# Mish between an attention's exponentials: fp16 products in place of 32-bit fused steps, with new thresholds for the order

## The chip, the cores and the metric

The kernel runs on one core of a Trainium2 chip. The metric is the device time of one execution in microseconds (us), as a median over runs. Shorter is better.

## The reference, cut to what matters

```python
x = A_x                                             # (1, 2048, 640), bf16
g = sigmoid((x * gate_w).sum(-1, keepdims=True))
# A: full attention, 32 heads of 20
q, k, v = heads(x @ wqkv)
a = softmax(q @ k.T * 20 ** -0.5) @ v @ wo
# B: dense layer with Mish
h = x @ w1 + b1                                     # 640 -> 1536
sp = log1p(exp(-abs(h))) + where(h > 0, h, 0)
b = (h * tanh(sp)) @ w2                             # 1536 -> 640
out = g * a + (1 - g) * b
```

Mish is `h * tanh(softplus(h))`. All of it is over 2048 tokens.

## The kernel before

**The bulk of the work** is attention: 2048 tiles of 128 keys by 512 queries (4 chunks of queries, 32 heads, 16 blocks of keys). TensorE forms the scores of three tiles at a time in one half of PSUM (a slot; two halves take turns, L1163), ScalarE turns them into exponentials in SBUF (`emit_e`, L1185), and TensorE multiplies these with V (`pv`, L1422). There are 683 such slots.

**The third tile of a slot can go to VectorE instead** ("off-loaded", `choose`, `emit_x`). ScalarE then takes 1024 elements per partition in place of 1536. VectorE evicts the third tile from PSUM as a scaled integer (L1230), and when four such tiles of a group have come together, `close` lines up three steps for the batch: an AND/OR for the fraction (L1294), a product in fp16 (L1298, often as two halves) and an AND/OR for the power (L1302). TensorE multiplies both parts of such a batch with V.

**Dense layer B.** Its first product is cut into 48 tasks (`h_task`), one for 256 tokens and 256 of the 1536 features. VectorE adds the bias as it evicts (L936). Two tasks make one call of `mish` on 128 x 1024 elements, 24 calls in all. ScalarE forms a tanh into a 32-bit buffer U (L959). Then VectorE forms a polynomial in U, times h, by four fused 32-bit steps of the form (in0 + constant) * in1 (SCALAR_TENSOR_TENSOR, L977), with the buffer U2 between them; the result replaces h. U has one copy (it moves from the tile W2R to the tile REG once). It is marked "busy" from the tanh to the last of the four steps, and the next call's tanh is only issued after that. A factor MISH_BY that the polynomial leaves out is in OMG, the factor (1 - g) by which the second product is scaled (L992).

**The order of all instructions is worked out in Python** when the kernel is built, by the class `Plan` and the loop over slots at the end of `attention`. It keeps an estimated time for each engine, adds estimated costs (EXP, WIDE and so on), and decides greedily what comes next. Attention's slots have the lead. Tasks of the projections, of B and of the output are put between them on TensorE (`pick`, `put`); VectorE's work that isn't urgent stands in four kinds of queues (`norm`, two lanes of `soon` for the batches, `blend` for Mish, `bg`), and `work` takes what can begin first. `choose` off-loads a tile unless one of these stops it: VectorE's queue is over a bound (BEHIND, 8 us; after off-loaded slots in a row 5 and 4 us, and never four in a row), no buffer is free, or a batch could not be ready in time. The end of a batch is judged with the queue's length times CROWD. Tasks of B that lag behind their due slot by LAG or more bring the bound on the queue to SPARE (7 us).

The thresholds that the change touches: OWE (how much background work of TensorE may be owed before more is put between), STREAM (below which share of work TensorE repeats scores to stay busy), SPREAD (over how many slots a task with a deadline is spread), GAP (the wait before scores from which a task is put there), CROWD, EAGER (how far ahead of its due slot a task is taken when others can't run), MISH (VectorE's cost of a Mish per task, for the check of what must end in time), LAG and REFILL (how long before ScalarE needs them the next scores must be due).

Of the kernel before, what the change touches and what calls it, by code (L numbers as in the profile page):

```python
# [12 lines left out]
FP16 = mybir.dt.float16  # L13
AF = mybir.ActivationFunctionType
ALU = mybir.AluOpType
# [14 lines left out]
CW = 512  # L30
# [6 lines left out]
NETS = 6  # L37
OLD = 3
WAITED = 3
OWE = 0.6  # L40
SLOT = 3
PV_HOLD = 2
HALF = D // 2
# [9 lines left out]
COL = 1 / 2400.0  # L53
PASS = CW * COL
EXP = 1.335
STREAM = 0.48
SPUN = 0.65
EXP_PAIR = 0.908
WIDE = 0.60
FAST = 0.335  # L60
HALVED = 0.41
HALF_WORK = 0.6
# [14 lines left out]
QUAD = 0.60  # L77
DOUBLE = 1.134
AHEAD = 14
SPREAD = 2  # L80
GAP = 0.5
SLOW_LOAD = 5.0
EARLY = 4
BEHIND = 8
PATIENCE = 5
CATCH_UP = 5
BUSY = 0.6
CROWD = 1.6
MARGIN = 2.5
EAGER = 20  # L90
LOAD = 0.95
MISH = 2.25
GROUP = 2.2
LAST = 0
END = 45
SHIFT = 0.4
LAG = 25
SPARE = 7
WINDOW = 3.41
CALM = 3  # L100
# [6 lines left out]
H_AT = 150  # L107
H_STEP = 12.5
THIN = 0.09
REFILL = 0.66  # L110
OVER = 0.2
CUTS = ((0, 256), (256, 256))

# [5 lines left out]
ULPS = 1024 / math.log(2)  # L119
BIAS = 15 * 1024 + 436  # L120
LIFT = math.log(1.5069154) + 436 / ULPS
MISH_STEPS = (1.5274980615848066, -5.90257334954394, 18.967422148121276, -6.430071830749512)
MISH_BY = -0.006540836794009846
MISH_AT = 0.6830045149697055
MANTISSA = 0x3FF
EXPONENT = 0x7C00
HALVES = 0x3800
# [111 lines left out]
def bass_gated_mix__softmax_full_mha__dense_activation_mish__prompt_kernel(  # L239
# [19 lines left out]
    def sb(name, shape, dt):  # L259
        return st.enter_context(nc.sbuf_tensor(name, shape, dt))  # L260
# [20 lines left out]
    U2 = sb("U2", [P, 2 * CW], FP32)  # L281
# [8 lines left out]
    GATE = sb("GATE", [P, NTB], FP32)  # L290
    OMG = sb("OMG", [P, NTB], FP32)
# [90 lines left out]
    def attention(pl, fast):  # L382
# [56 lines left out]
        def dve(fn, deps=(), cost=0.1, kind="F"):  # L439

            ready = max([pl.now["dve"], *(d.t1 + HOP for d in deps if d is not None)])
            work(ready + (LATER if fast and now["rate"] < BUSY and now["bank"] else SLACK))
            return pl.add("dve", fn, deps, cost=cost, kind=kind)
# [72 lines left out]
        if fast:  # L516
# [73 lines left out]
            def kq_task(k, g, c, due, forced=True):  # L590
# [8 lines left out]
                def finish(bank, last):  # L599
# [4 lines left out]
                    to = dst[:, g, c * CW:(c + 1) * CW]  # L604
                    ev = dve(lambda e: e.tensor_copy(to, PS[:, bank, :]), [last], WIDE)
                    (q_done, k_done)[k][(g, c)] = ev
# [21 lines left out]
            def shelve(k, name, c, rows, src, ev, n, i=0):  # L628

                done = (q_done, k_done)[k]  # L630
                written[(k, name, c)] = moved = pl.add(
                    "sp", lambda e: e.dma_start((QS, KS)[k].ap()[c, rows, :], src), [ev], f"{'qk'[k]}w{n}{i}", cost=0.5)
                (wq_read, k_moved)[k].append(moved)
                stage_free.setdefault((k, n), []).append(moved)
                for g, names in needs_of.items():
                    if (g, c) not in done and name in names and all((k, m, c) in written for m in names):
                        done[(g, c)] = None
                        later(now["step"] + 3, lambda g=g, c=c, names=names: fetch(k, g, c, names))
# [20 lines left out]
            def pack_task(k, i, c, due):  # L659
# [8 lines left out]
                def finish(bank, last):  # L668
# [4 lines left out]
                    to = stages[k][n]  # L673
                    ev = dve(lambda e: e.tensor_copy(to, PS[:, bank, :]), [last, *stage_free.pop((k, n), ())], WIDE)
                    shelve(k, i, c, slice(base, base + P), to, ev, n)
# [9 lines left out]
            def pack_end_task(k, c, due):  # L685
# [9 lines left out]
                def finish(bank, last):  # L695
# [5 lines left out]
                    to = stages[k][n]  # L701
                    ev = dve(lambda e: e.tensor_copy(to, PS[:, bank, :]), [last, *stage_free.pop((k, n), ())], WIDE)
                    for i in range(2):
# [14 lines left out]
            def copy(eng, dst, src, dep, cost):  # L718
                if eng == "act":
                    return pl.add("act", lambda e: e.copy(dst, src), [dep], cost=cost + 0.04)  # L720
                return pl.add("dve", lambda e: e.tensor_copy(dst, src), [dep], cost=cost)
# [8 lines left out]
            def first_keys():  # L730
# [3 lines left out]
                def turn(f):  # L734
# [4 lines left out]
                    turned[:] = [last]  # L739
                    moved[f] = bank_free[f] = copy(("dve", "act")[f % 2], xt(0)[:, f, :], PS[:, f, :], last, WIDE)  # L740

# [10 lines left out]
                q, k = QT[:, 0, 0:CW], KT[:, 0, 0:CW]  # L752
                q_done[(0, 0)] = bank_free[5] = copy("dve", q, PS[:, 5, :], last, WIDE)
                k_done[(0, 0)] = bank_free[FB] = copy("act", k[:, lows], PS[:, FB, 0:HW], low, 0.36)
# [37 lines left out]
            def v_pair_task(g, tiles, due):  # L792
# [9 lines left out]
                def finish(bank, last):  # L802
                    for c in cs:
# [5 lines left out]
                        V_all[:, tiles[0]:tiles[0] + m, g * HG:(g + 2) * HG, 1:EW],  # L809
                        got[:, :, 0:2 * HD].rearrange("p t (h d) -> p t h d", d=DH)), [last, m_one], WIDE * m / 3)  # L810
                    v_done.update({(g + i, t): ev for t in tiles for i in range(2)})
# [9 lines left out]
            def sigmoid(got):  # L821
                ex = pl.add("act", lambda e: e.activation(GATE[:, :], GT1[:, :], AF.Exp, scale=-1.0), [got], cost=0.2)
                a = dve(lambda e: e.tensor_scalar_add(OMG[:, :], GATE[:, :], 1.0), [ex])
                r = dve(lambda e: e.reciprocal(GATE[:, :], OMG[:, :]), [a], 0.25)
                gate_done.append(dve(lambda e: e.tensor_scalar(
                    OMG[:, :], GATE[:, :], -MISH_BY, MISH_BY, ALU.mult, ALU.add), [r]))

            grams = {}
            guarded = []
# [85 lines left out]
            h_done, b_read = {}, {}  # L915
            u_free = [None]

            def h_task(hc, k, due):
# [25 lines left out]
                def ready():  # L944
                    if len(acts) > 1 or not guarded or n1 not in w1_load or (hc >= 2 and len(b_read.get(hc - 2, ())) < 4):
                        return None
                    if hc == 1 and not back(("h", 0)):
# [3 lines left out]
                return Task([mm(i, f) for i in range(2) for f in range(NFT)], HW * COL, finish, due, ready,  # L951
                            dve=WIDE + MISH)

            def mish(ev, hb, hc, k):


                h = hb.rearrange("p i t -> p (i t)")
                U = AREAS[6 * hc + k >= FIRST][2]
                ex = pl.add("act", lambda e: e.activation(U, h, AF.Tanh, scale=0.5, bias=-MISH_AT / 2), [ev, u_free[0]], cost=0.95)  # L959
                u_free[0] = "busy"  # L960
                last = [ex]
                due = ex.t1 + PATIENCE

                def piece(cost, fn, after=None):
                    def run():
                        last[0] = pl.add("dve", fn, [last[0]], cost=cost)
                        if after:
                            after(last[0])
                    blend.append((cost, run, lambda: last[0], due))

                def done(op):
                    u_free[0] = h_done[(hc, k - 1)] = h_done[(hc, k)] = op

                two = 2 * WIDE - 0.07
                steps = ((U2[:, :], U, U), (U2[:, :], U2[:, :], U), (U, U2[:, :], h), (h, U2[:, :], U))
                for n, (to, one, by) in enumerate(steps):
                    piece(two, lambda e, n=n, to=to, one=one, by=by: e.scalar_tensor_tensor(  # L977
                        to, one, MISH_STEPS[n], by, ALU.add, ALU.mult), done if n == 3 else None)

            def b_task(hc, t, half, due):  # L980
                c, part = divmod(hc, 2)
# [139 lines left out]
        def emit_s(s):  # L1121
# [7 lines left out]
            if fast and s >= EARLY:  # L1129
                ready = max(d.t1 + HOP for d in deps if d is not None)  # L1130
                while ready - pl.now["pe"] > GAP:
                    t = pick(ready)
# [191 lines left out]
        def choose(s):  # L1324
# [8 lines left out]
            def tight(group, need):  # L1333
                ends = max((i for i, v in enumerate(near) if v[:2] == group), default=0)
                left = ends / TAKEN * EXP
                before = sum(t[0] for t in blend if t[3] < pl.now["act"] + left)
                return (late + urgent + before) * CROWD + need + MARGIN >= left

# [187 lines left out]
        if fast:  # L1526
# [64 lines left out]
            done = 0.0  # L1591
# [39 lines left out]
        def pick(limit):  # L1631
# [7 lines left out]
            for t in tasks:  # L1639
                if begin + t.cost > limit or passed and t.due > now["step"] + EAGER:  # L1640
                    return None
# [30 lines left out]
        def room():  # L1672
# [4 lines left out]
            owing = sum(t.dve for t in tasks) + sum(t[0] for todo in (norm, *soon, blend, bg) for t in todo)  # L1677
            owing += 2 * MISH * len(acts) + GROUP * (len(order) // (NKT * HG) + 1) + CHAIN
            return owing + max(0.0, pl.now["dve"] - pl.now["act"]) < LOAD * (NSLOT - LAST - step) * EXP
# [25 lines left out]
        def fill_up(to_come, last):  # L1705
# [3 lines left out]
            while step < NSLOT and pl.streamed(upto - WINDOW) + to_come < SPUN * WINDOW:  # L1709
                short = pl.streamed(upto - WINDOW) + to_come < STREAM * WINDOW  # L1710
                free = bank_free.get(FB)
# [9 lines left out]
        for step in range(NSLOT + 40):  # L1721
# [3 lines left out]

            for t in [t for t in tasks if t.forced and t.due - SPREAD <= step]:
                share = t.left() / (max(0, t.due - step) + 1)
# [33 lines left out]
            if step + 2 < NSLOT:  # L1761
                compose(step + 2, choose(step + 2) if fast and step >= CALM and (step < slot_of(0, 1, 0) or behind < CATCH_UP and (lag < LAG or backlog() < SPARE) and room()) else None)
                emit_s(step + 2)
# [9 lines left out]
            if fast and step + 2 < NSLOT:  # L1773
                latest[0] = pl.now["act"] + sum(EXP_PAIR if s in off else EXP for s in (step + 1, step + 2)) - REFILL
                limit = min(limit, latest[0])
# [9 lines left out]

            while owed > (OWE if turn and fast and step < NSLOT else 0):
                t = pick(limit)
# [35 lines left out]
        for n, (bank, t, half) in enumerate(jobs):  # L1823
            tb = c * 4 + t
            dst = ended(t, half)
# [138 lines left out]
```

## Time and profile before

| | |
|---|---|
| median of 3 runs | 800.76 us (800.62 to 800.96) |
| the profiled execution | 800.83 us; its span in the trace 799.0 us |
| granted TensorE clock, mean | 0.997 |
| slots with three tiles on ScalarE / with two | 303 / 380 |
| Mish calls (tanh on ScalarE) | 24 |

How to read the lines that follow: a line names the kernel's line (L1185), the engine, the operation, the tile written and the tiles read, with partitions x elements and type, then a count, the time busy and the mean duration of one. PE is TensorE, PEld its weight loads, ACT ScalarE, DVE VectorE, SP the engine that issues most DMAs. A duration in the trace includes a start and an end that overlap with the neighbours on the same engine; the time that an instruction takes up is read from the distance of two starts.

### The profile page before, as it was taken

The numbers are of one execution on the slowest core, as the hardware profiler recorded it, in microseconds if no ns is written. First come the engines' busy times: TensorE is split into PE (matmuls) and PEld (weight loads), VectorE is DVE, ScalarE is ACT, GpSimd is POOL, SyncE is SP. The second block draws the span as 40 slices with busy tenths as digits, with TensorE's granted clock in tenths as the row PEclk, the third lists the DMA queues.
The fourth block names the chain that finished last, engine by engine and source line by source line (L and its number), as shares of the span: only waits on it lengthen the run. The fifth ranks groups of instructions, "written<-read, shape, count | busy, mean of one in ns | idle before, by whom it ended". The sixth has DMA issues, their size and how long they took to land.

```text
span 799.0 us, 16266 instructions
## 1 busy us (share of the span) xinstructions
PE 722.8 (90%) x6665; PEld 261.2 (33%) x6665; DVE 739.9 (93%) x1195; ACT 782.0 (98%) x714; POOL 7.3 (1%) x14
## 2 busy tenths in 40 slices
PE   8899999999988889999999989989889888989995
PEld 3333333233322333233323333333333333333332
DVE  4798989999999999989999989999899999999995
ACT  6999999999999999999999999999999999999995
POOL 3000000000000000000000000000000000000000
PEclk9999999999999999999999999999999999999998
DMA  9731310122233212401112113120131212110101
GB/s 219 100 69 50 105 51 15 49 78 62 60 89 101 76 53 76 132 20 47 43 26 60 48 35 94 47 80 15 36 100 48 81 39 61 28 28 23 28 16 39
DMA packets 78182, 48.49 MB, mean 61 GB/s; under 512 B 23964, under 2 KB 73748, under 8 KB 78052
## 3 DMA queue, kind: packets, MB, share of 16 engines
q1 hardware_dynamic: 75732, 46.87, 22.6%
q8 instruction: 56, 0.92, 0.5%
q10 hardware_dynamic: 2256, 0.47, 0.3%
q0 software_dynamic: 112, 0.01, 0.1%
q14 instruction: 26, 0.21, 0.1%
HBM read 37.64 MB, written 7.52 MB: 57 GB/s over the span
## 4 chain that ended last, share of the span: by engine, by line
ACT 94%; PE 2%; DMA 2%; SPq 1%; DVE 1%; issue 0%
ACT ETS L1185 91%; ACT REG L959 2%; DMA XB<-in_A_x_dram 2%; SPq L531 1%; ACT W2R L959 1%; PE PS L1163 1%; PE PS L1422 0%; PE PS L798 0%; PE PS L596 0%; DVE HB L1015 0%; SPq L558 0%; PE PS L1009 0%; DVE KT L1230 0%; SPq L525 0%; DVE HB L936 0%
## 5 line engine op out<-in xcount | busy, mean ns | idle before, releaser
L1185 ACT ACTIVATE ETS<-PS 128x1024 bf16<-128x1024 f32 (+1 forms) x683 | 764.6, 1457 | 2.1 <-PE PS L1163 2.1
L1163 PE MATMUL PS<-QT,KT 32*128 32x512 bf16 (+1 forms) x2126 | 269.1, 377 | 60.6 <-ACT ETS L1185 51.2
L1422 PE MATMUL PS<-ETS,V_all 128*21 128x512 bf16 (+1 forms) x1722 | 166.9, 375 | 0.0
L1163 PEld LDWEIGHTS PS<-QT,KT 32*128 32x128 bf16 x2126 | 67.3, 91 | 287.8 <-ACT ETS L1185 261.7
L985 PE MATMUL PS<-W2R,HB 128*128 128x320 bf16 x384 | 69.4, 302 | 1.1 <-DVE XB L992 0.9
L1230 DVE TENSOR_SCALAR QT<-PS 128x512 int16<-128x512 f32 x87 | 59.6, 685 | 9.1 <-PE PS L1163 8.2
L1422 PEld LDWEIGHTS PS<-ETS,V_all 128*21 128x21 bf16 x1722 | 42.5, 90 | 43.1 <-issue 29.4
L1230 DVE TENSOR_SCALAR PADS<-PS 128x512 int16<-128x512 f32 x79 | 53.8, 685 | 2.8 <-PE PS L1163 2.6
L1230 DVE TENSOR_SCALAR OTN<-PS 128x512 int16<-128x512 f32 x77 | 52.4, 681 | 2.2 <-PE PS L1163 2.1
L926 PE MATMUL PS<-XB,REG 128*128 128x256 bf16 x360 | 53.1, 274 | 1.2 <-DVE OUTT L1015 0.4
L985 PEld LDWEIGHTS PS<-W2R,HB 128*128 128x128 bf16 x384 | 30.2, 97 | 34.3 <-issue 20.4
L926 PEld LDWEIGHTS PS<-XB,REG 128*128 128x128 bf16 x360 | 29.4, 97 | 24.3 <-issue 21.8
L1230 DVE TENSOR_SCALAR KT<-PS 128x512 int16<-128x512 f32 x46 | 31.3, 685 | 4.1 <-PE PS L1163 4.0
L936 DVE TENSOR_TENSOR HB<-PS,B1T 128x512 bf16<-128x512 f32 x48 | 32.8, 684 | 0.3
L1230 DVE TENSOR_SCALAR REG<-PS 128x512 int16<-128x512 f32 x40 | 27.2, 683 | 0.8 <-PE PS L1163 0.6
L1009 PE MATMUL PS<-WOQ,QT 128*128 128x320 bf16 x128 | 24.1, 302 | 2.1 <-DVE QT L1497 0.9
L1702 PE MATMUL PS<-KT 128*128 128x512 bf16 x82 | 24.8, 384 | 0.0
L798 PE MATMUL PS<-REG,XB 128*128 128x160 bf16 (+1 forms) x240 | 22.9, 234 | 1.3 <-DVE OUTT L813 1.0
L1009 PE MATMUL PS<-WOQ,OTN 128*128 128x320 bf16 x128 | 23.1, 302 | 0.5 <-DVE OUTT L1015 0.4
L665 PE MATMUL PS<-XB,WOQ 128*128 128x512 bf16 x80 | 23.5, 384 | 0.0
L959 ACT ACTIVATE REG<-HB 128x1024 f32<-128x1024 bf16 x18 | 23.4, 1303 | 0.0
L665 PE MATMUL PS<-XB,REG 128*128 128x512 bf16 x80 | 23.4, 384 | 0.0
(194 smaller groups left out, 834.7 us busy)
## 6 DMA issues: line engine op xcount, KB each, us to landing
REG<-in_B_w_dram SPq DMA_DIRECT2D x36, 320.0 KB, 3.2
BCT<-SUMS SPq DMA_DIRECT2D x124, 64.0 KB, 2.1
W2R<-in_B_w_dram SPq DMA_DIRECT2D x12, 320.0 KB, 3.6
KT<-KS SPq DMA_DIRECT2D x28, 128.0 KB
QT<-QS SPq DMA_DIRECT2D x112, 20.0 KB
QS<-WOQ SPq DMA_DIRECT2D x16, 128.0 KB, 1.8
KS<-OTN SPq DMA_DIRECT2D x16, 128.0 KB, 1.7
W2R<-in_B_w_dram SPq DMA_DIRECT2D x1, 1920.0 KB, 8.1
```

The lines of the kernel that those rows point to most:

```text
L665: return lambda e, bank: e.matmul(PS[:, bank, :], W[:, f, base:base + P], xt(c)[:, f, :], start=(f == 0), stop=(f == NFT - 1))
L798: return lambda e, bank: e.matmul(PS[:, bank, i * n:(i + 1) * n], xt(t // 4)[:, f, t % 4 * P:(t % 4 + 1) * P], WV[:, f, g * HD:g * HD + n] ...
L926: return lambda e, bank: e.matmul(PS[:, bank, i * HW:(i + 1) * HW], w1b(n1)[:, f, i * P:(i + 1) * P], xt(c)[:, f, cols], start=(f == 0), s ...
L936: ev = dve(lambda e: e.tensor_tensor(hb, PS[:, bank, :].rearrange("p (i t) -> p i t", i=2), bias, ALU.add), [last, b_load, *guarded, *b_re ...
L959: ex = pl.add("act", lambda e: e.activation(U, h, AF.Tanh, scale=0.5, bias=-MISH_AT / 2), [ev, u_free[0]], cost=0.95)
L985: return lambda e, bank: e.matmul(PS[:, bank, 0:HALF], HB[:, hc % 2, f, t * P:(t + 1) * P], W2[:, f, half * HALF:(half + 1) * HALF], start ...
L1009: return lambda e, bank: e.matmul(PS[:, bank, 0:HALF], otn(c, g, fast)[:, t * P:(t + 1) * P], WOG[:, g, half * HALF:(half + 1) * HALF], st ...
L1163: op = pl.add("pe", lambda e, i=i, g=real(g), tile=tile, j=j, cols=cols, c=c, of_q=of_q: e.matmul(scores(s)[:, i, cols], KT[32 * j:32 * j ...
L1185: e_op[s] = pl.add("act", lambda e: e.activation(ETS[:, s % NETS, 0:n, :], scores(s)[:, 0:n, :], AF.Exp, scale=SCALE, bias=LIFT if fast el ...
L1230: ev = dve_by(lambda e: e.tensor_scalar(block(batch["y"], n, I16), scores(s)[:, 2, :], SCALE * ULPS, BIAS, ALU.mult, ALU.add), [s_op[s], * ...
L1422: lasts[n] = pl.add("pe", lambda e, v=v, j=j, src=src[:, cols], of_q=of_q, count=count: e.matmul(PS[32 * j:32 * j + EW, ACC, of_q], v, src ...
L1702: pl.add("pe", lambda e: e.matmul(PS[:, bank, :], k[:, 0:P], k, start=True, stop=True), [free], cost=PASS, kind="S")
```

## The change

The polynomial gets another form. With t the tanh, w = t + 1, p = w (w + c1), q = (p + c2)^2, Mish is taken as h w (a q + b). The steps are single-operand additions and multiplications (tensor-scalars) and products of two tensors, all with fp16 operands behind the first, which reads the 32-bit U. The two fp16 buffers W and B lie in U2's two halves. U is given free by the first step. The polynomial's factor is no longer in OMG, which becomes 1 - g. Nine thresholds get other values; QUICK is the order's estimate for one of the new short steps.

```diff
-OWE = 0.6
+OWE = 0.2
-STREAM = 0.48
+STREAM = 0.5
+QUICK = 0.335
-SPREAD = 2
-GAP = 0.5
+SPREAD = 3
+GAP = 0.3
-CROWD = 1.6
+CROWD = 1.4
-EAGER = 20
+EAGER = 30
-MISH = 2.25
+MISH = 2.0
-LAG = 25
+LAG = 5
-REFILL = 0.66
+REFILL = 0.58
-MISH_STEPS = (1.5274980615848066, -5.90257334954394, 18.967422148121276, -6.430071830749512)
-MISH_BY = -0.006540836794009846
-MISH_AT = 0.6830045149697055
+MISH_AT = 0.213084983
+MISH_IN = -0.730890085
+MISH_MID = -5.619519
+MISH_OUT = 32.2033795
+MISH_BY = 0.0119979529
...
-                    OMG[:, :], GATE[:, :], -MISH_BY, MISH_BY, ALU.mult, ALU.add), [r]))
+                    OMG[:, :], GATE[:, :], -1.0, 1.0, ALU.mult, ALU.add), [r]))
...
-                ex = pl.add("act", lambda e: e.activation(U, h, AF.Tanh, scale=0.5, bias=-MISH_AT / 2), [ev, u_free[0]], cost=0.95)
+                ex = pl.add("act", lambda e: e.activation(U, h, AF.Tanh, scale=0.5, bias=-MISH_AT), [ev, u_free[0]], cost=0.95)
...
+                def read(op):
+                    u_free[0] = op
+
                 def done(op):
-                    u_free[0] = h_done[(hc, k - 1)] = h_done[(hc, k)] = op
-
-                two = 2 * WIDE - 0.07
-                steps = ((U2[:, :], U, U), (U2[:, :], U2[:, :], U), (U, U2[:, :], h), (h, U2[:, :], U))
-                for n, (to, one, by) in enumerate(steps):
-                    piece(two, lambda e, n=n, to=to, one=one, by=by: e.scalar_tensor_tensor(
-                        to, one, MISH_STEPS[n], by, ALU.add, ALU.mult), done if n == 3 else None)
+                    h_done[(hc, k - 1)] = h_done[(hc, k)] = op
+
+                W, B = (U2[:, n * CW:(n + 1) * CW].bitcast(FP16) for n in range(2))
+
+                def scalar(dst, src, one, two=None):
+                    ops = (one, two, ALU.mult, ALU.add) if two is not None else (one, None, ALU.add)
+                    return lambda e: e.tensor_scalar(dst, src, *ops)
+
+                def times(dst, one, two):
+                    return lambda e: e.tensor_tensor(dst, one, two, ALU.mult)
+
+                piece(WIDE, scalar(W, U, 1.0), read)
+                piece(QUICK, scalar(B, W, MISH_IN))
+                piece(WIDE, times(B, W, B))
+                piece(QUICK, scalar(B, B, MISH_MID))
+                piece(WIDE, times(B, B, B))
+                piece(QUICK, scalar(B, B, MISH_BY, MISH_BY * MISH_OUT))
+                piece(WIDE, times(B, W, B))
+                piece(WIDE, times(h, B, h), done)
```

## The prediction

> **What bounds the kernel.** I read the engines' busy time first, then the chain that ended last.
>
> ```profile
> span 799.0 us, 16266 instructions
> PE 722.8 (90%) x6665; PEld 261.2 (33%) x6665; DVE 739.9 (93%) x1195; ACT 782.0 (98%) x714; POOL 7.3 (1%) x14
> ACT 94%; PE 2%; DMA 2%; SPq 1%; DVE 1%; issue 0%
> ```
>
> ScalarE is busy all the time and 94% of the chain is its own. So the time is ScalarE's work, plus a start and an end of which the change has nothing. The profiled execution took 800.83 us, 1.83 more than its span and 0.07 more than the median of 800.76; I count from 800.83. What ScalarE's work consists of shows in its groups by shape, and what each instruction takes up in its order of time:
>
> ```profile
> L1185 ACT ACTIVATE ETS<-PS 128x1536 bf16<-128x1536 f32 x303 | 496.4, 1694 | 1.1 <-PE PS L1163 1.1
> L1185 ACT ACTIVATE ETS<-PS 128x1024 bf16<-128x1024 f32 x380 | 438.8, 1268 | 1.0 <-PE PS L1163 1.0
> L959 ACT ACTIVATE REG<-HB 128x1024 f32<-128x1024 bf16 x18 | 23.4, 1303 | 0.0
> ...
> 600.62 2.54 ACT L1185 ACTIVATE ETS<-PS 128x1024 bf16<-128x1024 f32 x2
> 601.52 2.55 ACT L1185 ACTIVATE ETS<-PS 128x1536 bf16<-128x1536 f32 x2
> 602.85 2.57 ACT L1185 ACTIVATE ETS<-PS 128x1024 bf16<-128x1024 f32 x2
> ```
>
> All 683 exponentials waited 2.1 us in sum (the numbers behind the bar): ScalarE has no gaps to close. Its time falls only if a slot goes from three tiles to two. That is worth 1694 - 1268 = 426 ns by the durations, and 1.33 - 0.90 = 0.43 by the starts (601.52 to 602.85, 600.62 to 601.52). 380 of 683 slots are there already. The price of one more is VectorE's time, so I looked at whether VectorE has any, by stages:
>
> ```profile
> 32.00:116.00 84.00, 78.31 (x802) 29.34 (x801) 73.87 (x124) 83.72 (x78) 0.00 (x0) 1.00 0.31 69
> 152.00:300.00 148.00, 133.41 (x1208) 46.73 (x1208) 141.82 (x226) 148.00 (x135) 0.00 (x0) 1.00 0.26 74
> 300.00:450.00 150.00, 140.89 (x1203) 44.48 (x1203) 142.49 (x229) 150.00 (x142) 0.00 (x0) 1.00 0.21 57
> 450.00:600.00 150.00, 136.42 (x1214) 51.91 (x1211) 142.36 (x221) 150.00 (x136) 0.00 (x0) 1.00 0.21 58
> 600.00:708.00 108.00, 96.23 (x854) 36.88 (x852) 106.94 (x161) 108.00 (x97) 0.00 (x0) 1.00 0.18 47
> 708.00:788.00 80.00, 73.38 (x775) 26.52 (x775) 75.33 (x135) 80.00 (x74) 0.00 (x0) 1.00 0.09 24
> ```
>
> The columns after the length are PE, PEld, DVE and ACT. From 152 to 788 ScalarE is busy 100% and VectorE 94% to 99%, with 27.1 us idle in all (6.2, 7.5, 7.6, 1.1 and 4.7). So both engines are full, and the order shares the exponentials between them. VectorE time that is saved anywhere here is worth time only by being spent again on off-loaded tiles. Mish's steps (the first of a call, the last, and the busy time of all in two stages) lie inside this stretch:
>
> ```profile
> L977 DVE SCALAR_TENSOR_TENSOR U<-W2R x6: 1215/1216/1218, 168.6 to 318.8; 128x1024 f32<-128x1024 f32 x6
> L977 DVE SCALAR_TENSOR_TENSOR HB<-U,REG x18: 1215/1215/1219, 401.7 to 719.7; 128x1024 bf16<-128x1024 f32 x18
> ...
> 450.00:600.00 150.00, 35.27 (x29) 1.00 0.21 58
> 600.00:708.00 108.00, 37.64 (x31) 1.00 0.18 47
> ```
>
> **The change part by part: Mish's steps.** VectorE's groups by shape, and its order of time:
>
> ```profile
> L1230 DVE TENSOR_SCALAR QT<-PS 128x512 int16<-128x512 f32 x87 | 59.6, 685 | 9.1 <-PE PS L1163 8.2
> L977 DVE SCALAR_TENSOR_TENSOR REG<-U,HB 128x1024 f32<-128x1024 f32 x18 | 21.9, 1217 | 0.1
> L977 DVE SCALAR_TENSOR_TENSOR HB<-U,REG 128x1024 bf16<-128x1024 f32 x18 | 21.9, 1216 | 0.0
> L1302 DVE TENSOR_SCALAR QT<-QT 128x2048 int16<-128x2048 int16 x20 | 13.7, 685 | 0.2
> L1298 DVE TENSOR_TENSOR OTN<-OTN 128x1024 f16<-128x1024 f16 x13 | 8.8, 681 | 0.0
> L1302 DVE TENSOR_SCALAR OTN<-OTN 128x1024 int16<-128x1024 int16 x4 | 1.7, 420 | 0.0
> L1294 DVE TENSOR_SCALAR OTN<-OTN 128x2048 int16<-128x2048 int16 x7 | 4.8, 687 | 0.0
> ...
> 600.37 0.68 DVE L1230 TENSOR_SCALAR OTN<-PS 128x512 int16<-128x512 f32 x1
> 600.97 1.22 DVE L977 SCALAR_TENSOR_TENSOR U<-U,REG 128x1024 f32<-128x1024 f32 x1
> 602.11 0.62 DVE L1302 TENSOR_SCALAR REG<-REG 128x1024 int16<-128x1024 int16 x2
> ```
>
> Starts lie 0.60 apart behind an instruction of 0.68, and 1.14 behind one of 1.22: 0.08 overlaps with the next. Removed are four fused steps: 4 x (1.216 - 0.08) = 4.54 us for each of 24 calls. Added are eight:
> - Three fp16 products in place of 1024 elements like L1298's: 0.681, so 0.60 each.
> - Three fp16 additions or multiply-adds: like L1302's row with 1024 two-byte elements, 0.420, so 0.34 each.
> - The first step, 32-bit to fp16 from SBUF. No row has one. Bounds: 0.68, the row with the same bytes read in the same kind of instruction (L1302, 2048 x 2 bytes), and 1.22, one element at a time as in L977's row. I take 0.68, so 0.60, since its operation is the same.
> - The last product, fp16 times bf16. No row mixes the two; bounds 0.68 (L1298) and 1.22 (L977). I take 0.68, so 0.60: all operands have two bytes, as in L1298.
>
> Sum 5 x 0.60 + 3 x 0.34 = 4.02 us, so 0.52 less; 24 x 0.52 = 12.5 us less VectorE work. At both upper bounds it would be 2 x 0.54 = 1.08 more, 5.10 us, and the change a loss of 13.4 us of VectorE.
>
> For the first step the Trainium skill has a price ("VectorE: DVE Perf Modes", section "The perf-mode tier table"): a tensor-scalar of 2048 32-bit elements in SBUF takes 1227 ns at two elements a cycle, by which 1024 would take an estimated 0.69 us; no run here shows that, and the sum would stay where it is.
>
> **What 12.5 us buy.** One off-loaded tile costs VectorE an eviction (0.685 - 0.08 = 0.605) and a quarter of a batch: (0.607 + 2 x 0.60 + 0.605) / 4 = 0.60; together 1.21. It saves ScalarE 0.426, and as both engines must end together, VectorE's stretch becomes shorter by as much. So n x (1.21 + 0.426) = 12.5 gives n = 7.6 tiles, and 7.6 x 0.426 = 3.3 us.
>
> **U given free early.** A tanh waits in the order until the last step of the call before it:
>
> ```profile
> 607.32 1.29 ACT L959 ACTIVATE REG<-HB 128x1024 f32<-128x1024 bf16 x1
> ...
> 618.29 1.22 DVE L977 SCALAR_TENSOR_TENSOR HB<-U,REG 128x1024 bf16<-128x1024 f32 x1
> ...
> 620.82 1.37 ACT L959 ACTIVATE REG<-HB 128x1024 f32<-128x1024 bf16 x1
> ```
>
> Here that is 618.29, and the next tanh starts at 620.82. With the change U is free after the first step, some 10 us earlier. The tanh costs ScalarE the same wherever it is, and exponentials cover the wait, so I put this at nothing for itself; were that cover gone, ScalarE would lose the wait. What is late next is Mish's work on VectorE, which stays in order in its queue. The gain is that B lags less, and that two calls can stand in the queue, so that a step that waits for the step before it finds other work ahead. No wait and no DMA is added; steps stay in the same queues. The tanh's bias and OMG are constants: nothing.
>
> **The thresholds.** They move TensorE's tasks earlier or closer to the scores (OWE, GAP, EAGER, SPREAD, REFILL, STREAM) and let batches stay open longer (CROWD), while LAG holds VectorE's queue to 7 us in place of 8 more often. Bounds: at best half of VectorE's idle time, 27.1 from 152 to 788 and 10.1 from 32 to 116, turns into tiles; 18.6 / 1.636 x 0.426 = 4.8 us gained. At worst scores come late to ScalarE:
>
> ```profile
> PEld PS L1163 <- ACT ETS L1185: 261.7, 562, 1.2
> ACT ETS L1185 <- PE PS L1163: 2.1, 5, 0.6
> ```
>
> 562 times of 683 slots the scores' weights wait for ScalarE, so TensorE is early; in the other 121 it isn't. If each of these loses the 0.08 us by which REFILL falls, that is 9.7 us lost. The row that I stand nearer to is VectorE's idle time, as ScalarE's own waits are only 2.1 us, and I take a quarter of the upper bound: 1.2 us gained.
>
> **Sum:** 800.83 - 3.3 - 1.2 = 796.3 us. A change within 0.2% (1.6 us) counts as none: that is about what a measurement of this kernel can tell.
>
> **The rivals.**
>
> *The fixed part of eight steps eats the saving.* If each step waits for the whole of the one before it, the durations count in full: 4 x 1.216 = 4.86 against 5 x 0.68 + 3 x 0.42 = 4.66, so 0.20 saved a call, 4.8 us in all, 1.3 us by the same division: 799.5. Against it: in the order of time other work stands on both sides of Mish's step, and the starts overlap. They also leave little that is fixed in an instruction: 1.14 us for 1024 elements against 0.60 for 512 leaves 0.06. Chance 0.11. The Trainium skill speaks for this rival ("VectorE: DVE Perf Modes", section "Rules for kernel authors"): of chained operations it says to minimize their count, since each empties the pipeline before the next, and here the count doubles; by the starts above the trace does not bear that out as a large cost.
>
> *The time isn't spent again.* The rules on the queue's length, on four tiles in a row or on buffers hold the count near 380, and VectorE gets idle time: 800.8. Against it: VectorE's queue is what most of these rules look at, and it gets shorter. Chance 0.05.
>
> *Scores late for ScalarE: slower.* Tighter REFILL and GAP let a task's matmuls run into the time for the scores. The price is above: 0.08 us in 121 slots, 9.7 us, so 800.83 - 3.3 + 9.7 = 807.2; at 41 slots it eats the 3.3. For it: PE is busy 89% to 94% in the stages. Against it: in 562 slots there is room. Chance 0.08.
>
> *One element at a time in the first step and the last: slower.* The order then counts on 4.02 us for what takes 5.10: 26 us that it doesn't know of, 16 of them in the 60 steps, 15 calls, from 450 to 708, where VectorE is idle 7.6 + 1.1 = 8.7. Some 7 us overrun, no tile given back: 796.3 + 7 = 803.3. It decides once the first or last step shows 1.2 us. Chance 0.04.
>
> **How the numbers follow.** The forecast has 0.72, its own range 792 to 799: from the 3.3 with the whole 4.8 (792.7) to half of the 3.3 alone (799.2). The first rival (0.11) I split, 0.03 faster, 0.08 the same; with the second's 0.05 that is 0.13 the same. Slower is 0.08 + 0.04 = 0.12, faster 0.75. The range reaches from 791 (those 792.7, and 1.7 for steps that find other work ahead, which I can't price closer) to 802, which takes in the two middle rivals and the mild end of late scores.
>
> **What would show it.** Right: tensor-scalars of 0.42 and 0.68, products of 0.68 in Mish's line, 24 of each step, some 4.0 us of starts a call; 388 to 396 exponentials of 128x1024 in place of 380; VectorE as busy as before; ScalarE's waits for scores near 2 us; tanhs that start before the last step of the call ahead. Wrong: a count of 380 or less, a step of 1.2 us, or waits of ScalarE above 5 us.

## The result and the profile after

The changed kernel takes 795.23 us (median of 6 runs, 794.3 to 796.0) against 800.86 (6 runs, 800.35 to 801.73); the ratio is 0.9929, 95% interval 0.9916 to 0.9942. So it is 5.6 us faster where 4.5 were forecast. The profiled execution took 796.0 us. Its page, engines and chain:

```profile
span 794.1 us, 16410 instructions
PE 714.3 (90%) x6648; PEld 263.3 (33%) x6686; DVE 739.6 (93%) x1313; ACT 776.7 (98%) x714; POOL 7.3 (1%) x14
ACT 89%; DVE 4%; PE 3%; DMA 2%; SPq 1%; issue 0%
```

ScalarE still sets the end, with 5.3 us less to do, and VectorE is as busy as before with 118 instructions more. The groups by shape of ScalarE and of Mish on VectorE:

```profile
L1203 ACT ACTIVATE ETS<-PS 128x1536 bf16<-128x1536 f32 x290 | 459.6, 1625 | 0.8 <-PE PS L1181 0.8
L1203 ACT ACTIVATE ETS<-PS 128x1024 bf16<-128x1024 f32 x393 | 432.2, 1197 | 1.0 <-PE PS L1181 1.0
...
L987 DVE TENSOR_TENSOR U<-U 128x1024 f16<-128x1024 f16 x72 | 48.9, 679 | 0.1
L984 DVE TENSOR_SCALAR U<-U 128x1024 f16<-128x1024 f16 x72 | 29.9, 415 | 0.2
L987 DVE TENSOR_TENSOR HB<-U,HB 128x1024 bf16<-128x1024 f16 x24 | 16.4, 682 | 0.1
L984 DVE TENSOR_SCALAR U<-REG 128x1024 f16<-128x1024 f32 x18 | 12.3, 683 | 0.0
```

There are 393 slots with two tiles, 13 more than before. 13 x 0.426 = 5.5 us, which is the gain. ScalarE's waits for scores stay small (0.8 + 1.0 us). VectorE in the stages (the fifth column, ScalarE in the sixth):

```profile
152.00:300.00 148.00, 132.32 (x1226) 47.30 (x1239) 146.17 (x259) 148.00 (x137) 0.00 (x0) 1.00 0.26 76
300.00:450.00 150.00, 138.85 (x1213) 46.16 (x1216) 144.30 (x248) 149.66 (x142) 0.00 (x0) 1.00 0.20 56
450.00:600.00 150.00, 137.27 (x1226) 51.87 (x1226) 146.69 (x269) 150.00 (x138) 0.00 (x0) 1.00 0.19 53
600.00:708.00 108.00, 96.92 (x865) 37.48 (x866) 106.95 (x192) 107.75 (x99) 0.00 (x0) 1.00 0.19 53
```

VectorE's idle time from 152 to 708 is 1.8 + 5.7 + 3.3 + 1.1 = 11.9 us; before it was 6.2 + 7.5 + 7.6 + 1.1 = 22.4. Behind 708 it is the other way, 3.0 us before and 7.7 after (VectorE alone, the kernel before and then the changed one):

```profile
708.00:780.00 72.00, 68.96 (x120) 1.00 0.10 26
```
```profile
708.00:780.00 72.00, 64.26 (x118) 1.00 0.07 19
```

Over the whole span VectorE is idle 59.1 us before (799.0 - 739.9) and 54.5 after (794.1 - 739.6). So it is as busy as before, since Mish's saving went into tiles, and idle 4.6 us less, about as much as the span is shorter.

### The profile page after: what moved, and what is told of

The parts are those of the page before. It is cut to its first block, busy times and chain, and to the rows that moved or that the text cites. A ratio compares the mean times of both kernels' runs of the same rounds, so it can differ in the third digit from the quotient of the medians.

```text
span 794.1 us, 16410 instructions
## 1 busy us (share of the span) xinstructions
PE 714.3 (90%) x6648; PEld 263.3 (33%) x6686; DVE 739.6 (93%) x1313; ACT 776.7 (98%) x714; POOL 7.3 (1%) x14
## 4 chain that ended last, share of the span: by engine, by line
ACT 89%; DVE 4%; PE 3%; DMA 2%; SPq 1%; issue 0%
ACT ETS L1203 86%; ACT REG L962 2%; DMA XB<-in_A_x_dram 2%; SPq L534 1%; PE PS L1440 1%; PE PS L1181 1%; ACT W2R L962 1%; DVE OTN L1248 1%; DVE U L987 0%; DVE OTN L1316 0%; DVE U L984 0%; PE PS L1027 0%; DVE HB L1033 0%; PE PS L599 0%; DVE OTN L1312 0%
## 5 line engine op out<-in xcount | busy, mean ns | idle before, releaser
L1181 PE MATMUL PS<-QT,KT 32*128 32x512 bf16 (+1 forms) x2127 | 269.7, 378 | 60.0 <-ACT ETS L1203 51.1
L1181 PEld LDWEIGHTS PS<-QT,KT 32*128 32x128 bf16 x2127 | 67.8, 91 | 281.4 <-ACT ETS L1203 256.1
L1248 DVE TENSOR_SCALAR QT<-PS 128x512 int16<-128x512 f32 x97 | 66.1, 684 | 1.7 <-PE PS L1181 1.2
L987 DVE TENSOR_TENSOR U<-U 128x1024 f16<-128x1024 f16 x72 | 48.9, 679 | 0.1
L1248 DVE TENSOR_SCALAR KT<-PS 128x512 int16<-128x512 f32 x52 | 35.4, 683 | 4.6 <-PE PS L1181 4.3
L1248 DVE TENSOR_SCALAR REG<-PS 128x512 int16<-128x512 f32 x48 | 32.8, 683 | 1.4 <-PE PS L1181 1.3
L984 DVE TENSOR_SCALAR U<-U 128x1024 f16<-128x1024 f16 x72 | 29.9, 415 | 0.2
L1720 PE MATMUL PS<-KT 128*128 128x512 bf16 x77 | 23.3, 384 | 1.3 <-issue 1.1
L1522 DVE COPY OUNG<-PS 128x512 f32<-128x512 f32 x31 | 21.2, 683 | 2.8 <-PE PS L1440 2.6
```

Source lines behind the costliest of these rows:

```text
L984: return lambda e: e.tensor_scalar(dst, src, *ops)
L987: return lambda e: e.tensor_tensor(dst, one, two, ALU.mult)
L1181: op = pl.add("pe", lambda e, i=i, g=real(g), tile=tile, j=j, cols=cols, c=c, of_q=of_q: e.matmul(scores(s)[:, i, cols], KT[32 * j:32 * j ...
L1248: ev = dve_by(lambda e: e.tensor_scalar(block(batch["y"], n, I16), scores(s)[:, 2, :], SCALE * ULPS, BIAS, ALU.mult, ALU.add), [s_op[s], * ...
```

## The experiments

Theory: the time is the count of two-tile slots at 0.426 us each; Mish's saved VectorE time buys the tiles. Rivals: the thresholds alone did it; the early release of U did it; VectorE's time is worth something without tiles. From the fifth run on the theory has a second term, what the order leaves behind the last exponential.

The table splits each profiled span: start of the first exponential to start of the last ("stretch"), and from there to the span's end ("end"). Medians are of the timed runs; the kernel before, beside them, took 800.51, 800.67 and 800.73 in the three sets (runs 1 to 4, 5 to 8, 9 to 12). Where the last column is 0.995 or less (runs 3, 5, 6, 9 and 10), the granted TensorE clock was at half for 8 us or more near the end of that profile, so its end isn't the order's alone.

| kernel | median, us | two-tile slots | stretch | end | granted clock of the profiled run |
|---|---|---|---|---|---|
| before | 800.86 | 380 | 778.7 | 10.2 | 0.997 |
| changed | 795.23 | 393 | 773.1 | 10.7 | 0.999 |
| 1 Mish alone | 800.06 | 387 | 775.3 | 12.0 | 0.999 |
| 2 thresholds alone | 802.31 | 380 | 778.1 | 12.1 | 0.999 |
| 3 U held | 797.41 | 394 | 773.0 | 12.3 | 0.995 |
| 4 old cost told | 802.09 | 380 | 777.4 | 11.2 | 0.999 |
| 5 first step thrice | 808.52 | 372 | 783.7 | 12.8 | 0.993 |
| 6 U in fp16 | 800.11 | 388 | 778.3 | 11.2 | 0.991 |
| 7 old lead of TensorE | 798.00 | 384 | 776.0 | 10.2 | 0.997 |
| 8 old queue rules | 795.51 | 391 | 772.8 | 10.0 | 0.998 |
| 9 U held, short end | 796.28 | 393 | 773.6 | 12.9 | 0.992 |
| 10 long end | 798.03 | 393 | 772.7 | 13.2 | 0.993 |
| 11 U in fp16, new order | 791.28 | 406 | 768.6 | 9.9 | 0.996 |
| 12 new order only | 793.90 | 395 | 771.9 | 10.0 | 0.998 |

The counts named in the first four expectations are one too high each; the traces show those of the table.

**1, Mish alone.** The changed kernel with these lines back at their old values:

```diff
-OWE = 0.2, STREAM = 0.5, SPREAD = 3, GAP = 0.3, CROWD = 1.4, EAGER = 30, MISH = 2.0, LAG = 5, REFILL = 0.58
+OWE = 0.6, STREAM = 0.48, SPREAD = 2, GAP = 0.5, CROWD = 1.6, EAGER = 20, MISH = 2.25, LAG = 25, REFILL = 0.66
```

> Mish's new steps with all nine old thresholds. The order that comes out has 388 slots with two tiles (before: 380, the changed kernel: 393). My theory, that freed VectorE time becomes off-loaded tiles at 0.43 us of ScalarE each: 8 tiles, 3.4 us faster than before, 797.4 us, so some 60% of the change's gain. Rival 'the thresholds did it': no faster than 800.8. Rival 'early release of U did it': as the changed kernel, 795.2, since U is released early here too.

Measured 800.06 against 800.51, ratio 1.0 (0.9991 to 1.0009): no gain that can be told. Yet 7 tiles were added and the stretch is 3.4 us shorter, as the theory has it. The end is 1.8 us longer and gave half of it back (the rest lies ahead of the first exponential and outside the span, where each profiled run differs by some tenths). Nor was all of Mish's saving spent:

```profile
span 797.5 us, 16359 instructions
PE 716.4 (90%) x6640; PEld 260.9 (33%) x6681; DVE 732.7 (92%) x1288; ACT 778.9 (98%) x714; POOL 7.3 (1%) x14
```

VectorE is idle 797.5 - 732.7 = 64.8 us, 5.7 more than before. Its order behind the last exponential shows what lies in the end:

```profile
787.64 0.45 DVE L1509 STREAM_TRANSPOSE BCT<-PS 128x256 f32<-128x256 f32 x1 [0.45 <-PE PS L1440]
788.13 0.20 DVE L1510 RECIPROCAL RR<-BCT 128x8 f32<-128x8 f32 x1
788.37 0.45 DVE L1511 STREAM_TRANSPOSE BCT<-RR 128x256 f32<-128x256 f32 x1
788.85 0.42 DVE L1515 TENSOR_TENSOR QT<-PS,BCT 128x256 bf16<-128x256 f32 x1
789.19 0.54 DVE L1033 SCALAR_TENSOR_TENSOR HB<-PS,GATE,W2R 128x320 bf16<-128x320 f32 x1
790.27 0.55 DVE L1033 SCALAR_TENSOR_TENSOR HB<-PS,GATE,W2R 128x320 bf16<-128x320 f32 x1 [0.54 <-PE PS L1027]
791.30 1.47 DVE L1033 SCALAR_TENSOR_TENSOR HB<-PS,GATE,W2R 128x320 bf16<-128x320 f32 x3 [0.48 <-PE PS L1027]
```

L1509 to L1515 are the last normalisation. Two output tasks (L1033 at 789.19 and 790.27) come behind it one by one, 1.08 us apart, and the second and the last three wait for their products (the brackets). In the changed kernel these lines follow one another:

```profile
786.43 0.42 DVE L1515 TENSOR_TENSOR QT<-PS,BCT 128x256 bf16<-128x256 f32 x1
786.77 2.09 DVE L1033 SCALAR_TENSOR_TENSOR HB<-PS,GATE,W2R 128x320 bf16<-128x320 f32 x4
```

**2, thresholds alone.** The kernel before with the nine new values (the diff of run 1 the other way).

> The old fused Mish steps with all nine new thresholds. The order has 381 slots with two tiles, one more than before. My theory: 800.4 us, less than 0.2% from before, since no VectorE time is freed. Rival 'the thresholds did it': near 795.2. Rival 'scores late': slower than before by more than 1.6 us, with waits of ScalarE for scores above 5 us.

Measured 802.31, ratio 1.0024 (1.0015 to 1.0033): slower. No tile is added and the stretch is the same to 0.7 us; the end is 1.9 us longer, again with two output tasks one by one. ScalarE's waits for products of TensorE before an exponential are 1.4 us in sum, so it isn't late scores. The rival "the thresholds did it" falls, and so does my 800.4: tiles alone don't give the time.

**3, U held.** U is given free by the last step:

```diff
-                piece(WIDE, scalar(W, U, 1.0), read)
+                piece(WIDE, scalar(W, U, 1.0))
...
-                    h_done[(hc, k - 1)] = h_done[(hc, k)] = op
+                    u_free[0] = h_done[(hc, k - 1)] = h_done[(hc, k)] = op
```

> The changed kernel, but U is given free only by the last of the eight steps, as before the change. The order has 395 slots with two tiles. My theory: the release is worth nothing by itself, 794.4 us by the count of tiles (two more than the changed kernel), within 0.2% of it. Rival 'early release of U did it': back to 798 or more.

Measured 797.41, 2.2 us over the changed kernel and 3.0 over the expectation. The stretch is that of the changed kernel; the end isn't. VectorE has a batch there (L1312 to L1320) ahead of the last normalisation, which the changed kernel hasn't:

```profile
784.96 0.42 DVE L1312 TENSOR_SCALAR OTN<-OTN 128x1024 int16<-128x1024 int16 x1
785.41 0.69 DVE L1316 TENSOR_TENSOR OTN<-OTN 128x1024 f16<-128x1024 f16 x1
786.13 0.43 DVE L1320 TENSOR_SCALAR OTN<-OTN 128x1024 int16<-128x1024 int16 x1
787.29 0.45 DVE L1509 STREAM_TRANSPOSE BCT<-PS 128x256 f32<-128x256 f32 x1 [0.73 <-PE PS L1440]
```

Runs 9 and 10 tell what that is worth.

**4, old cost told.** The same instructions, but the order counts 4.52 us for a call:

```diff
+TOLD = 0.064
...
-                piece(WIDE, scalar(W, U, 1.0), read)
-                piece(QUICK, scalar(B, W, MISH_IN))
+                piece(WIDE + TOLD, scalar(W, U, 1.0), read)
+                piece(QUICK + TOLD, scalar(B, W, MISH_IN))
...
```

> The changed kernel's instructions for Mish, but the order is told that each of the eight steps costs 0.064 us more, so that a call costs it 4.52 us as before. The order has 381 slots with two tiles. VectorE does the work faster than the order thinks. My theory: the saved VectorE time isn't spent, so 800.3 us with some 12 us more of VectorE's idle time. Rival 'shorter Mish is worth time by itself' (fewer late evictions, less waiting): 797 or less at the same count.

Measured 802.09, ratio 1.002 (1.0011 to 1.0029). With the count at 380 none of the gain is left, though Mish takes VectorE less time than before. From 152 to 708 VectorE's idle time is 7.0 + 8.9 + 7.4 + 3.9 = 27.2 us, 4.8 more than before (VectorE alone):

```profile
152.00:300.00 148.00, 141.02 (x245) 1.00 0.25 69
300.00:450.00 150.00, 141.08 (x244) 1.00 0.23 62
450.00:600.00 150.00, 142.63 (x253) 1.00 0.19 53
600.00:708.00 108.00, 104.08 (x187) 1.00 0.19 51
```

Over the whole span it is 799.0 - 730.8 = 68.2 us, 9.1 more than before, where I had expected 12. Run 2 is the nearest kernel: the same thresholds, the same 380 tiles, the old Mish. VectorE is busy 739.8 us there, 9.0 more than here, and the kernel took 802.31, only 0.2 us more. So the rival "a shorter Mish is worth time by itself" falls; at most 0.7 us of the stretch (778.1 to 777.4) could be its.

**5, first step thrice.**

```diff
+                piece(WIDE, scalar(W, U, 1.0))
+                piece(WIDE, scalar(W, U, 1.0))
                 piece(WIDE, scalar(W, U, 1.0), read)
```

> The changed kernel with Mish's first step done three times in place of once (the same values again), and the order is told: 2 x 0.60 us x 24 = 28.9 us more VectorE work. By the division of my prediction that is 28.9 / 1.636 = 17.7 tiles fewer than 393; the order that comes out has 372 slots with two tiles, and it leaves one more output task behind the last normalisation than the changed kernel. Theory as it stands after the first four runs (time = tiles at 0.426 us + what the order leaves behind the last exponential): 800.7 at 380 tiles with a short end, + 8 x 0.43 + 1.6 = 805.7 us. Rival 'the count is only a mark and VectorE's work has cover': 797 or less, near the changed kernel.

Measured 808.52, ratio 1.0096 (1.008 to 1.0111). 28.9 us more on VectorE cost 21 tiles (18 by division), and the time follows, 2.8 us beyond the expectation. Two waits of ScalarE ahead of the exponentials at 256.4 and 260.9, of 1.0 and 1.1 us (1.3 and 1.2 by the distances of starts), and the end of 12.8, partly at half the clock, account for it.

**6, U in fp16.**

```diff
-                U = AREAS[6 * hc + k >= FIRST][2]
+                U = AREAS[6 * hc + k >= FIRST][2][:, 0:CW].bitcast(FP16)
...
-                piece(WIDE, scalar(W, U, 1.0), read)
+                piece(QUICK, scalar(W, U, 1.0), read)
```

> The changed kernel, but ScalarE writes the tanh as fp16 and the first step reads it so: 0.34 us in place of 0.60, 6.2 us less VectorE work in all. By the prediction's division 3.8 tiles more and 1.6 us faster, 793.6. But the order that comes out has only 388 slots with two tiles, 5 fewer than the changed kernel, with a short end. Theory of tiles and end: 800.7 - 8 x 0.43 = 797.3 us, slower than the changed kernel although VectorE has less to do. Rival 'freed VectorE time is worth time however it is spent': 793.6.

Measured 800.11 (798.93 to 802.07). VectorE has 6.2 us less to do, and the kernel is 4.9 us slower than the changed one: the order made of it 5 tiles fewer, some 2.1 us. The other 2.9 us are one wait of ScalarE ahead of the exponential at 331.9 (2.5 us of idle time, 2.9 by the distance of starts), where TensorE's order of time shows filler matmuls (L1720) between two slots' scores (L1181):

```profile
327.14 0.39 PE L1181 MATMUL PS<-QT,KT 32*128 32x512 bf16 x3
327.47 4.06 PE L1720 MATMUL PS<-KT 128*128 128x512 bf16 x18
331.46 0.39 PE L1181 MATMUL PS<-QT,KT 32*128 32x512 bf16 x4
```

The order filled this time with 18 such matmuls, which by the code it does up to the time at which it expects ScalarE to go on. What it had down as late here isn't followed.

**7, old lead of TensorE; 8, old queue rules.** The changed kernel with six thresholds back, and with the other three:

```diff
7: OWE = 0.6, STREAM = 0.48, SPREAD = 2, GAP = 0.5, EAGER = 20, REFILL = 0.66
8: CROWD = 1.6, LAG = 25, MISH = 2.25
```

> The changed kernel with the old values of the six thresholds that place TensorE's background work (OWE, STREAM, SPREAD, GAP, EAGER, REFILL), the new ones of CROWD, LAG and MISH. The order has 384 slots with two tiles and a short end. Theory of tiles and end: 800.7 - 4 x 0.43 = 799.0 us. Rival 'CROWD and LAG are what matters': 795.2.

> The changed kernel with the old values of CROWD, LAG and MISH, the new ones of the six thresholds that place TensorE's background work. The order has 391 slots with two tiles and a short end. Theory of tiles and end: 800.7 - 11 x 0.43 = 796.0 us. Rival 'CROWD and LAG are what matters': 799 or more. Rival 'the six cost ScalarE late scores': more than 2 us over the theory, with ScalarE's waits above those of the changed kernel.

Measured 798.00 (ratio 0.9967, 0.9955 to 0.9979) and 795.51 (0.9935, 0.9922 to 0.9949): both within 1 us of the expectation. Of the thresholds the six that lead TensorE's work carry it, CROWD, LAG and MISH hardly anything. VectorE's idle time over the whole span is 63.4 us in run 7 (796.7 - 733.3) and 52.4 in run 8 (792.9 - 740.5), beside 54.5 in the changed kernel.

**9, U held, short end; 10, long end.**

```diff
9 (over run 3):       END = 45  ->  END = 44
10 (over changed):    LAST = 0  ->  LAST = 2
```

> U held to the last of the eight steps, as in the third run, and END at 44 in place of 45, which gives an order with 393 slots with two tiles, as the changed kernel, and no batch left for the end. Theory: the release of U is worth nothing by itself, and the third run's 2.2 us over the changed kernel were its end; so 795.5 us, within 0.2% of the changed kernel. Rival 'the release has a worth of its own': 797.4 again.

> The changed kernel with LAST at 2 in place of 0: VectorE's order is the same for its first 1266 rows and has 393 slots with two tiles too, but behind the last exponential stand 11 steps of VectorE in place of 8, three of them of a batch. Theory of tiles and end: 2 us slower than the changed kernel, 797.2, and all of it behind the last exponential. Rival 'the end has slack': 795.2.

Run 9 took 796.28, 1.05 us from the changed kernel (0.13%), so the early release is worth nothing that can be told and hardly more than 1 us: in four of its five executions the mean clock was lower (0.992 to 0.996) than any of the changed kernel's, and the one at 0.999 took 796.17. Run 10 took 798.03 at the same count, 2.8 us over the changed kernel, its stretch not longer: the end has no slack. VectorE's order there shows a batch (L1312 to L1320) ahead of the last normalisation:

```profile
784.18 0.55 DVE L1033 SCALAR_TENSOR_TENSOR HB<-PS,GATE,W2R 128x320 bf16<-128x320 f32 x1 [0.79 <-PE PS L1027]
784.65 0.42 DVE L1312 TENSOR_SCALAR OTN<-PADS 128x1024 int16<-128x1024 int16 x1
785.10 0.69 DVE L1316 TENSOR_TENSOR OTN<-OTN,PADS 128x1024 f16<-128x1024 f16 x1
785.83 0.43 DVE L1320 TENSOR_SCALAR PADS<-PADS 128x1024 int16<-128x1024 int16 x1
787.39 0.45 DVE L1509 STREAM_TRANSPOSE BCT<-PS 128x256 f32<-128x256 f32 x1 [1.14 <-PE PS L1440]
```

Run 9, without run 3's batch in its end, is 1.1 us faster than run 3; run 10, with such a batch, is 2.8 us slower than the changed kernel.

Part of both runs' ends in the profile isn't the order's (the profiled execution of run 9 was its slowest, 798.55). The granted clock (the third number from the right) fell during them, here run 9 and then run 10, and not in the changed kernel's:

```profile
780.00:788.00 8.00, 7.11 (x81) 0.53 0.11 33
```
```profile
780.00:788.00 8.00, 5.63 (x69) 0.82 0.11 33
```

The runs of one kernel bear this out: run 10 took 796.85 to 797.31 where the mean clock was 0.997 and 797.89 to 799.36 at 0.993 to 0.996. Against the changed kernel's 795.23, at a mean clock of 0.998 to 0.999, the former are 1.6 to 2.1 us slower, about the 2 that were expected.

**11, U in fp16, new order; 12, new order only.** Other values for the order's estimates and bounds:

```diff
11 (over run 6):    WAITED = 2, STREAM = 0.46, SLACK = 0.2, FILL = 2.0, IDLE = 6, AHEAD = 10, BEHIND = 7, PATIENCE = 12,
                    BUSY = 0.7, CROWD = 1.3, LOAD = 0.97, SHIFT = 0.5, LAG = 0, SPARE = 6, REFILL = 0.54, OVER = 0.3
12 (over changed):  WAITED = 4, OWE = 0.3, PATIENCE = 3, BUSY = 0.7, LOAD = 0.93, MISH = 2.25, END = 40, SHIFT = 0.5,
                    LAG = 25, SPARE = 8, OVER = 0.3
```

> The tanh in fp16, as in the sixth run, and 16 of the order's thresholds set anew for it. The order has 406 slots with two tiles (the changed kernel 393) and a short end of 8 steps. Theory of tiles and end: 800.7 - 26 x 0.43 = 789.5 us. The 6.2 us of VectorE that fp16 frees give only 4 tiles by the prediction's division; the other 9 must come from VectorE's idle time. Rival 'VectorE has no more idle time to give': its steps run behind the order, ScalarE waits for buffers or scores, and the time is 794 or more.

> The changed kernel's instructions with another 11 of the order's thresholds set anew. 395 slots with two tiles, short end. Theory of tiles and end: 800.7 - 15 x 0.43 = 794.3 us. Rival 'between orders of nearly the same count the waits decide': off by more than 1.6 us.

Run 11 took 791.28 (ratio 0.9889, 0.9874 to 0.9904), the fastest of all, and run 12 793.90 (0.9918, 0.9904 to 0.9931). Run 11 is 1.8 us over the expectation, run 12 0.4 under it. So what run 6 seemed to say of fp16 was its order, not fp16. VectorE's idle time is 41.7 us in run 11 (788.6 - 746.9), 12.8 less than in the changed kernel, so the rival "no more idle time to give" falls. How much of run 11's gain is fp16's isn't separated from its thresholds, which aren't run 12's. Run 11's groups on ScalarE:

```profile
L1203 ACT ACTIVATE ETS<-PS 128x1024 bf16<-128x1024 f32 x406 | 432.6, 1163 | 0.3 <-PE PS L1181 0.2
L1203 ACT ACTIVATE ETS<-PS 128x1536 bf16<-128x1536 f32 x277 | 429.9, 1587 | 2.2 <-PE PS L1181 2.0
L962 ACT ACTIVATE REG<-HB 128x1024 f16<-128x1024 bf16 x18 | 22.1, 1226 | 0.0
```

## Why the prediction was right, and where it wasn't

**Mish's steps: right in every price.** The rows after show 683, 679, 415 and 682 ns; by the distances of starts (medians in the trace) that is 0.60, 0.60, 0.33 and 0.60, so 3.99 us a call where 4.02 stood. The estimate from the Trainium skill for the 32-bit first step ("VectorE: DVE Perf Modes", "The perf-mode tier table"), 0.69 us, agrees with the 0.683.

**What the saved time buys: right in tiles, wrong in time.** Run 1 has the 7 tiles (7.6 forecast) and 3.4 us in ScalarE's stretch (3.3 forecast). But only 0.45 us of it is in the median, no gain that can be told. The step that failed is "a start and an end of which the change has nothing": every new order ends in its own way. The ends of the experiments in whose profiles the final fall of the clock came only in the last 5 us (1, 2, 4, 7, 8, 11, 12) run from 9.9 to 12.1 us; that those of the kernels before and after the change lie only 0.5 us apart is luck, and it is why the sum came out. The 7 tiles are in part luck as well. Of some 13 us that Mish frees (24 x 0.54 by the starts) the evictions and batch steps took 6.9 (523.0 us busy against 516.1 before), so 1.0 a tile and not 1.21, while VectorE's idle time, which the division had as it was, rose by 5.7. In the changed kernel they are busy 532.4 us, 16.3 more for 13 tiles, 1.25 each: there the price was near.

**The thresholds: right in sign only together with Mish.** I had 1.2 us as a term of its own. By themselves they cost 1.8 us (802.31 against 800.51); on top of the new Mish they are worth 4.8 (800.06 to 795.23): 6 tiles, 2.6 us, and 1.3 us of the end, the rest not resolved. The terms don't add, and the total came out near by luck, since 3.3 was too much for Mish alone and 1.2 too little for the rest. The bound I worked out, idle time turned into tiles, was the right mechanism, but it works on what the new Mish leaves idle: from run 1 to the changed kernel VectorE's idle time falls by 10.3 us (64.8 to 54.5) and 6 tiles come. Against the kernel before it is 4.6 us less, near the quarter of the bound that I took (18.6 / 4 = 4.7).

**U given free early: right at nothing that can be told** (run 9), though tanhs do start early, as this call's on ScalarE ahead of the last steps of the call before it on VectorE. ("Some 10 us earlier" was rounded up: in the call that I showed the first step starts at 609.74 and the last at 618.29, 8.6 us apart.)

```profile
622.74 1.35 ACT L962 ACTIVATE REG<-HB 128x1024 f32<-128x1024 bf16 x1
```
```profile
629.62 0.68 DVE L987 TENSOR_TENSOR U<-U 128x1024 f16<-128x1024 f16 x1
630.34 0.69 DVE L987 TENSOR_TENSOR HB<-U,HB 128x1024 bf16<-128x1024 f16 x1
```

**The rivals.** The fixed part of eight steps: not as a whole, the starts lie 0.60 and 0.33 apart where other work stands between. But the mechanism is real: the last two lines above are steps of one call with nothing between them, and their starts lie 0.72 apart, the whole duration and 0.04 more. That happens behind 10 of the 168 steps that have a next one (0.71 to 0.72 in seven, 0.45 in the three short ones), some 1.2 us in all. So the count of operations, which the Trainium skill says to keep small ("VectorE: DVE Perf Modes", "Rules for kernel authors"), costs little in this trace. Time not spent again: not in the changed kernel, but run 1 spent only a part, run 4 brings it about, and run 6 shows that it happens by itself. Late scores: ScalarE waits 1.8 us for them. One element at a time: no step is near 1.2 us.

## What to carry to other kernels

Where two full engines share work, time saved on the helper is worth next to nothing (0.2 us between runs 2 and 4) until the order gives it more of the shared work: count the shared pieces in the trace, and price one of them on both engines. A greedy order made anew also ends anew, so measure the stretch and the end apart before a gain or a loss is put down to an instruction. Set the thresholds anew after the costs change, and not before: here the same nine values lost 1.8 us with the old costs, all of it in the end, and won 4.8 with the new.

## What the runs showed of the hardware that was not expected

The granted TensorE clock falls to half in the last microseconds, sooner or later from run to run (0.53 of full from 780 to 788 us in run 9's profile, 1.00 in the changed kernel's), though PE is busy 7.11 of those 8 us. The executions of the sixth kernel split by it: 798.93 to 800.45 us with a mean clock of 0.997 or 0.998, 801.42 to 802.07 with 0.991. So up to some 2 us go with it, as much as with a batch left for the end.

In these traces it falls behind thin work of TensorE. In the 3.4 us ahead of the fall PE is busy 2.04 us in run 9 (777.1 to 780.5), 2.02 in run 6 (781.6 to 785.0), 1.97 in run 10 (781.7 to 785.1) and 2.01 in run 11, where it fell once in the middle (619.0 to 622.4) and came back 3.4 us later; in the changed kernel it is 2.80 from 777.0 to 780.4, and the clock held. That is no sharp bound: run 5's clock fell behind 2.25 us (785.6 to 789.0), and run 8's held behind 2.15 (776.0 to 779.4). No experiment here thins TensorE's work by itself, so a cause is not shown.
